# Splitting the first loads over two DMA rings in a fused state-space and gated-MLP kernel

## The chip, the core and the metric

The kernel runs on one core of a Trainium2 chip. The metric is the device time of one execution in microseconds (us): the median of several timed runs. A profile of one further execution shows what each engine did: TensorE (PE for matmuls, PEld for the weight loads ahead of them), VectorE (DVE), ScalarE (ACT), GpSimd (POOL) and SyncE (SP). Two of these, SP and ACT, issue DMAs in this kernel; the rows of the profile call their issue queues SPq and ACTq, and each has a ring of its own that feeds the core's 16 DMA engines.

## What is computed

The input x has 2048 rows of 512 values in bf16. Each row is layer-normalised to xn, and three things are summed:

```
xn  = (x - mean) / sqrt(var + 1e-5)
A   = 2 * Re(scan(xn @ B_bar) @ C) + xn * Dskip      # complex diagonal recurrence over the rows
B   = (silu(xn @ w1) * (xn @ w3)) @ w2               # w1, w3: 512 x 1792; w2: 1792 x 512
out = x + A + B
```

B_bar and the recurrence's factors come from three parameter vectors of 512 values (Lambda_re, Lambda_im, log_dt).

## The kernel before, in words

The rows are cut into four blocks of 512, and each block into four row groups of 128 (`x_blk[b][:, c, :]`). A block passes through four stages on TensorE: `glu_up` (14 feature tiles f of w1 into `g_ps` and of w3 into `u_ps`, four matmuls each, one for each 128-wide slice dt of the 512 input values), `ssm_in`, and `y_out`, while VectorE works through a queue of tasks (normalising, the scan, products) and ScalarE empties PSUM. The order of everything is written by hand (`manual_schedule`): each engine runs its instructions in program order. SP also issues its DMAs in that order. The DMAs take eight completion semaphores in turn, so a DMA that gets a semaphore for the second time is issued only when the DMA before it on that semaphore has landed.

This case is about the first ten microseconds. There the first block has to be made ready in small steps:

- `load_rows` (L77) loads row groups of block 0. Rows 0 to 127 and 128 to 255 (128 KB each) are issued by SP, rows 256 to 511 (256 KB) by ACT.
- `load_w13(0, 4, 2)` (L95, called at L115) loads the columns of feature tiles 0 to 3 of w1 and w3 in four pieces of 256 KB, all on SP: w1 for dt 0 and 1 ("w1 low"), w1 for dt 2 and 3 ("w1 high"), then w3 low and w3 high. After these SP issues the columns of tiles 4 to 7, block 1 of x, the rest of w1 and w3, and so on.
- `load_prm` (L109) loads the three parameter vectors into `prm`, 1 KB each, on ACT.
- `keep_warm` (L150) runs matmuls on a constant; nothing reads their result. There are 8 with 512 columns and 5 with 128 ahead of the first real work, and 2 more with 128 columns between the transposes.
- `stats`, `aggr` (DVE, L164, L167), `rstd_act` (ACT, L171, L172) and `normed` (DVE, L192) normalise one row group; `turn` (PE, L251) transposes it in 128 x 128 pieces, and `put` (L256 on ACT, L258 on DVE) copies the transposed pieces from PSUM to `xnT`. The transposes of row group 1 use the PSUM tiles of feature tile 2 (`t1` is made of `begun[2]`).
- `ahead` (through `glu_mm`, L372) runs the matmuls of feature tiles 0, 1 and 2 on those row groups of block 0 that are ready, before `glu_up` finishes these tiles with the last row group.

On TensorE the order after the first dummies is: transposes of row group 0, two dummies, transposes of row group 1 (four: two low, two high), then

```
ahead((w1_sb,), B3, 0, 1, lo)          # w1 low,  row group 0, tiles 0 to 2: 6 matmuls of 128 columns
ahead((w1_sb,), B3, 1, 1, lo, True)    # w1 low,  row group 1: 6 of 128
ahead((w1_sb,), B3, 0, 2, hi)          # w1 high, row groups 0 and 1: 6 of 256
ahead((w3_sb,), B3, 0, 2, lo)          # w3 low:  6 of 256
turn(2, t2)
ahead((w3_sb,), B3, 0, 2, hi)          # w3 high: 6 of 256
```

followed by the transpose of `prm` (L544), row group 2, the transposes of row group 3, and the rest of `glu_up(0)`.

Of the kernel before, what the change touches and what calls it, by code (L numbers as in the profile page):

```python
# [16 lines left out]
P = 128  # L17
# [3 lines left out]
def kernel(  # L21
# [24 lines left out]
    nc = tc.nc  # L46
# [6 lines left out]
    CPB = TBLK // P  # L53
    NSB = TBLK // SB
    NDT = D // P
# [20 lines left out]
    def load_rows(c0, c1, eng):  # L76
        eng.dma_start(out=x_blk[0][:, c0:c1, :], in_=xv[:, 0, c0:c1, :])  # L77

    load_rows(0, 1, nc.sync)
    load_rows(1, 2, nc.sync)  # L80
    nc.scalar.preload_act_table_set("natural_log_exp_and_others")
    w1_sb = const.tile([P, NDT, F], BF16, name="w1_sb")
    w3_sb = const.tile([P, NDT, F], BF16, name="w3_sb")
    w2_sb = const.tile([P, NFT, D], BF16, name="w2_sb")
    w1v = B_w1.rearrange("(t p) f -> p t f", p=P)
    w3v = B_w3.rearrange("(t p) f -> p t f", p=P)

    H = NDT // 2

    def load_w13(f0, f1, parts=1):  # L90
        fs = slice(f0 * P, f1 * P)
        for w_sb, wv in ((w1_sb, w1v), (w3_sb, w3v)):
            for i in range(parts):
                ds = slice(i * NDT // parts, (i + 1) * NDT // parts)
                nc.sync.dma_start(out=w_sb[:, ds, fs], in_=wv[:, ds, fs])  # L95

    dskip_row = const.tile([P, D], BF16, name="dskip_row")
    bt = [const.tile([P, NDT, PS], BF16, name=f"bt{ri}") for ri in range(2)]
# [9 lines left out]
    def load_prm(i, src, eng):  # L108
        eng.dma_start(out=prm[i * NPT:(i + 1) * NPT, :], in_=src.rearrange("(t p) -> t p", p=P))  # L109

    load_prm(0, A_Lambda_re, nc.scalar)
    load_rows(2, CPB, nc.scalar)
    load_prm(1, A_Lambda_im, nc.scalar)
    load_prm(2, A_log_dt, nc.scalar)
    load_w13(0, 4, 2)  # L115
    load_w13(4, 8)
    nc.sync.dma_start(out=x_blk[1], in_=xv[:, 1, :, :])
    load_w13(8, NFT)
    nc.sync.dma_start(out=dskip_row, in_=A_Dskip.partition_broadcast(P))
    load_turned(bt[0], A_B_re)  # L120
# [26 lines left out]
    def keep_warm(n, width=512):  # L147
        one = nc.const_aps.tensor_like(1.0, like=ident[:, 0:1])
        for _ in range(n):
            nc.tensor.matmul(out=begun[0][0][:, :width], lhsT=one.to_broadcast([P, P]), rhs=one.to_broadcast([P, width]),  # L150
                             start=True, stop=True)

    keep_warm(8)
    keep_warm(5, P)


    mv_all = const.tile([P, NBLK * CPB, 2], FP32, name="mv_all")
# [4 lines left out]
    def stats(c):  # L162
        sums[c] = work.tile([P, 6], FP32, name="stats", bufs=4)
        nc.vector.bn_stats(out=sums[c], in_=x_blk[c // CPB][:, c % CPB, :])  # L164
# [4 lines left out]
    def rstd_act(c0, c1):  # L169
        y = rstd_all[:, c0:c1]  # L170
        nc.scalar.activation(out=y, in_=mv_all[:, c0:c1, 1], func=ACT.Ln, bias=LN_EPS)  # L171
        nc.scalar.activation(out=y, in_=y, func=ACT.Exp, scale=-0.5)  # L172
# [15 lines left out]
    def normed(c, parts=1):  # L188
        xn = work.tile([P, D], BF16, name="xn", bufs=8)
        for i in range(parts):  # L190
            ds = slice(i * D // parts, (i + 1) * D // parts)
            nc.vector.tensor_scalar(out=xn[:, ds], in0=x_blk[c // CPB][:, c % CPB, ds], scalar1=mv_all[:, c, 0:1],  # L192
                                    scalar2=rstd_all[:, c:c + 1], op0=ALU.subtract, op1=ALU.mult)
        return xn
# [54 lines left out]
    def turn(c, pxt, d0=0, d1=NDT):  # L249
        for dt in range(d0, d1):  # L250
            nc.tensor.transpose(out=pxt[:, dt - d0, :], in_=xn0[c][:, dt * P:(dt + 1) * P], identity=ident)  # L251

    def put(c, pxt, eng, d0=0, d1=NDT):
        dst = xnTs[0][:, d0:d1, c * P:(c + 1) * P]
        if eng is nc.scalar:
            nc.scalar.activation(out=dst, in_=pxt, func=ACT.Copy)  # L256
        else:
            nc.vector.tensor_copy(out=dst, in_=pxt)  # L258
# [110 lines left out]
    def glu_mm(b, f, w_sb, ps, ts, dts=range(NDT), joins=False):  # L369

        for dt in dts:
            nc.tensor.matmul(out=ps[:, ts], lhsT=w_sb[:, dt, f * P:(f + 1) * P], rhs=xnTs[b][:, dt, ts],  # L372
                             start=(dt == 0 and not joins), stop=(dt == NDT - 1))
# [128 lines left out]
    def ahead(w_sbs, fs, c, n=1, dts=range(NDT), joins=False):  # L502
        for f in fs:
            for w_sb in w_sbs:
                glu_mm(0, f, w_sb, begun[f][w_sb is w3_sb], slice(c * P, (c + n) * P), dts, joins)
# [13 lines left out]
    xn0[1] = normed(1, 2)  # L519
    turn(0, tb, H, NDT)  # L520
    put(0, tb, nc.scalar, H, NDT)
    keep_warm(2, P)
    turn(1, t1[0], 0, H)
    put(1, t1[0], nc.scalar, 0, H)
    turn(1, t1[1], H, NDT)
    put(1, t1[1], nc.scalar, H, NDT)
    stats(2)
    aggr(2)
    rstd_act(2, 3)
    stats(3)  # L530
    B3 = (0, 1, 2)
    lo, hi = range(H), range(H, NDT)
    ahead((w1_sb,), B3, 0, 1, lo)
    ahead((w1_sb,), B3, 1, 1, lo, True)
    ahead((w1_sb,), B3, 0, 2, hi)
    xn0[2] = normed(2)
    aggr(3)
    rstd_act(3, 4)
    ahead((w3_sb,), B3, 0, 2, lo)
    turn(2, t2)  # L540
    put(2, t2, nc.vector)
    xn0[3] = normed(3)
    ahead((w3_sb,), B3, 0, 2, hi)
    nc.tensor.transpose(out=pprm, in_=prm, identity=ident)  # L544
# [63 lines left out]
```

## Time and profile before

| | |
|---|---|
| median of 3 timed runs | 211.68 us (211.54 to 211.72) |
| the profiled execution | 212.11 us, of which the span from first to last instruction is 210.3 us |
| PE busy | 206.6 us, 98% of the span |
| DVE, ACT, POOL busy | 173.5, 93.4, 6.0 us |
| DMA | 13.69 MB, two rings (q1 is SP's with 13.24 MB, q10 is ACT's with 0.27 MB) |

In rows of the timeline the first number is the start in us from the begin of the span and the second is how long the group of instructions lasted; xN is how many there are. Where a wait preceded, it stands in brackets with what ended it. In the list of DMA issues the last number is the median time from the start of the issue to the landing of the last byte. Matmuls overlap: their starts tell the pace, while the duration of one is longer than the distance to the next.

### The profile page before, as it was taken

The numbers are of one execution on the slowest core, as the hardware profiler recorded it, in microseconds if no ns is written. First come the engines' busy times: TensorE is split into PE (matmuls) and PEld (weight loads), VectorE is DVE, ScalarE is ACT, GpSimd is POOL, SyncE is SP. The second block draws the span as 40 slices with busy tenths as digits, with TensorE's granted clock in tenths as the row PEclk, the third lists the DMA queues.
The fourth block names the chain that finished last, engine by engine and source line by source line (L and its number), as shares of the span: only waits on it lengthen the run. The fifth ranks groups of instructions, "written<-read, shape, count | busy, mean of one in ns | idle before, by whom it ended". The sixth has DMA issues, their size and how long they took to land.

```text
span 210.3 us, 2878 instructions
## 1 busy us (share of the span) xinstructions
PE 206.6 (98%) x1036; PEld 97.7 (46%) x1036; DVE 173.5 (82%) x346; ACT 93.4 (44%) x167; POOL 6.0 (3%) x27
## 2 busy tenths in 40 slices
PE   8999999999999999999999999999999999999994
PEld 3864444444444444444444444444444444444453
DVE  4699989989999999999999999999999999121111
ACT  3599967666666200066666600036666620000000
POOL 2010320000000000000000000000000000000000
PEclk9999999999999999999999999999999999999999
DMA  5999599944000000000004200100000000000110
GB/s 165 294 366 219 109 178 325 217 106 100 0 3 0 0 25 25 28 26 0 0 0 77 28 1 24 50 25 5 0 0 0 0 3 25 27 25 25 34 44 25
DMA packets 25014, 13.69 MB, mean 65 GB/s; under 512 B 15912, under 2 KB 25000, under 8 KB 25000
## 3 DMA queue, kind: packets, MB, share of 16 engines
q1 hardware_dynamic: 24704, 13.24, 26.1%
q10 hardware_dynamic: 296, 0.27, 0.4%
q8 instruction: 8, 0.13, 0.3%
q14 instruction: 6, 0.05, 0.1%
HBM read 7.74 MB, written 2.10 MB: 47 GB/s over the span
## 4 chain that ended last, share of the span: by engine, by line
PE 96%; DMA 2%; SPq 0%; DVE 0%; issue 0%
PE g_ps L372 23%; PE u_ps L372 23%; PE y_ps L488 23%; PE y_ps L493 13%; PE bu_ps L411 13%; DMA w_sb<-in_B_w_dram 2%; SPq L77 0%; PE xt_ps L251 0%; DVE o L498 0%; PE xt_ps L544 0%
## 5 line engine op out<-in xcount | busy, mean ns | idle before, releaser
L372 PEld LDWEIGHTS <-w_sb 128*128 128x128 bf16 x502 | 46.4, 98 | 50.6 <-DMA w_sb<-in_B_w_dram 0.6
L372 PE MATMUL g_ps<-xnT,w_sb 128*128 128x512 bf16 (+2 forms) x254 | 58.2, 354 | 0.3 <-DMA w_sb<-in_B_w_dram 0.3
L372 PE MATMUL u_ps<-xnT,w_sb 128*128 128x512 bf16 (+2 forms) x248 | 58.4, 358 | 0.0
L488 PE MATMUL y_ps<-w_sb,hgT 128*128 128x512 bf16 (+2 forms) x238 | 51.2, 366 | 0.0
L390 ACT ACTIVATE up<-u_ps 128x512 bf16<-128x512 f32 x56 | 34.0, 607 | 14.9 <-PE u_ps L372 14.9
L413 ACT ACTIVATE u<-bu_ps 128x512 bf16<-128x512 f32 x32 | 19.1, 597 | 46.3 <-PE bu_ps L411 46.3
L388 ACT ACTIVATE sl<-g_ps 128x512 bf16<-128x512 f32 x56 | 34.0, 608 | 9.9 <-PE g_ps L372 9.2
L445 DVE TENSOR_TENSOR_SCAN ab<-r_col,h,ab 128x256 bf16<-128x256 f32 x56 | 37.7, 733 | 0.2
L488 PEld LDWEIGHTS <-hgT 128*128 128x128 bf16 x238 | 22.8, 98 | 25.9
L498 DVE TENSOR_TENSOR o<-y_ps,x_blk 128x512 bf16<-128x512 f32 (+2 forms) x17 | 11.1, 654 | 24.3 <-PE y_ps L493 24.3
L493 PE MATMUL y_ps<-ct,h 128*128 128x512 bf16 (+2 forms) x136 | 30.4, 366 | 0.0
L411 PE MATMUL bu_ps<-xnT,bt 128*128 128x512 bf16 x128 | 28.1, 379 | 0.0
L397 DVE TENSOR_TENSOR hgT<-sl,up 128x512 bf16<-128x512 bf16 x56 | 22.9, 414 | 2.1 <-ACT up L390 2.1
L493 PEld LDWEIGHTS <-h 128*128 128x128 bf16 x136 | 13.0, 98 | 14.7
L411 PEld LDWEIGHTS <-bt 128*128 128x128 bf16 x128 | 12.5, 98 | 15.1
L164 DVE BATCH_NORM_STATS2 stats<-x_blk 128x6 f32<-128x512 bf16 x16 | 10.6, 675 | 2.5 <-DMA x_blk<-in_A_x_dram 2.5
L454 DVE TENSOR_TENSOR ab<-ab,tab_s 128x2048 bf16<-128x2048 bf16 x8 | 9.8, 1222 | 0.2
L450 DVE TENSOR_TENSOR ab<-ab,tab_c 128x2048 bf16<-128x2048 bf16 x8 | 9.8, 1222 | 0.1
L427 DVE TENSOR_TENSOR ab<-u,tab_x 128x2048 bf16<-128x2048 bf16 x8 | 9.7, 1219 | 0.0
L430 DVE TENSOR_TENSOR ab<-u,tab_y 128x2048 bf16<-128x2048 bf16 x8 | 9.7, 1218 | 0.0
L201 DVE TENSOR_TENSOR x_blk<-xd,x_blk 128x512 bf16<-128x512 bf16 x16 | 6.8, 426 | 0.5
L200 DVE TENSOR_TENSOR xd<-xn,dskip_row 128x512 bf16<-128x512 bf16 x16 | 6.7, 418 | 0.0
(76 smaller groups left out, 81.3 us busy)
## 6 DMA issues: line engine op xcount, KB each, us to landing
out_dram<-o SPq DMA_DIRECT2D x15, 128.0 KB, 1.7
w_sb<-in_B_w_dram SPq DMA_DIRECT2D x1, 1792.0 KB, 9.3
x_blk<-in_A_x_dram SPq DMA_DIRECT2D x3, 512.0 KB, 6.3
w_sb<-in_B_w_dram SPq DMA_DIRECT2D x2, 768.0 KB, 7.8
w_sb<-in_B_w_dram SPq DMA_DIRECT2D x4, 256.0 KB, 5.0
w_sb<-in_B_w_dram SPq DMA_DIRECT2D x2, 512.0 KB, 4.1
x_blk<-in_A_x_dram SPq DMA_DIRECT2D x2, 128.0 KB, 2.2
x_blk<-in_A_x_dram ACTq DMA_DIRECT2D x1, 256.0 KB, 4.7
```

The costliest lines, as they stand in the source:

```text
L164: nc.vector.bn_stats(out=sums[c], in_=x_blk[c // CPB][:, c % CPB, :])
L372: nc.tensor.matmul(out=ps[:, ts], lhsT=w_sb[:, dt, f * P:(f + 1) * P], rhs=xnTs[b][:, dt, ts], start=(dt == 0 and not joins), stop=(dt == ...
L388: nc.scalar.activation(out=sl16, in_=g_ps, func=ACT.Silu)
L390: nc.scalar.activation(out=up16, in_=u_ps, func=ACT.Copy)
L397: nc.vector.tensor_tensor(out=hg[b][:, f, :], in0=sl16, in1=up16, op=ALU.mult)
L411: nc.tensor.matmul(out=u_ps, lhsT=bt[ri][:, dt, pt * P:(pt + 1) * P], rhs=xnTs[b][:, dt, :], start=(dt == 0), stop=(dt == NDT - 1))
L413: nc.scalar.activation(out=u16[:, :, pt, ri, :], in_=u_ps.rearrange("p (s t) -> p s t", s=NSB), func=ACT.Copy)
L445: nc.vector.tensor_tensor_scan(out=a[:, pt, 2 * ri + 1, :], data0=r_b, data1=a[:, pt, 2 * ri, :], initial=init, op0=ALU.mult, op1=ALU.add)
L450: nc.vector.tensor_tensor(out=a[:, :, 0::2, :], in0=a[:, :, 1::2, :], in1=tab_b("c"), op=ALU.mult)
L488: nc.tensor.matmul(out=y_ps[:, ds], lhsT=hg[b][:, f, cl * P:(cl + 1) * P], rhs=w2_sb[:, f, ds], start=(f == 0), stop=False)
L493: nc.tensor.matmul(out=y_ps[:, ds], lhsT=h_tiles[i][:, pt, ri, h_ts], rhs=ct[ri][:, pt, ds], start=False, stop=(pt == NPT - 1 and ri == 1))
L498: nc.vector.tensor_tensor(out=o16[:, ds], in0=y_ps[:, ds], in1=x_blk[b][:, cl, ds], op=ALU.add)
```

## The change

Rows 128 to 255 are issued by ACT, ahead of its table load, and rows 256 to 511 by SP. ACT's ring then carries the two w1 pieces, SP's the two w3 pieces and after them the three parameter vectors. Five narrow dummies at the start become eight. On TensorE the w1 matmuls of tiles 0 and 1 are done for row group 0 first, the low half of them ahead of the high half of row group 1's transposes; tile 2 comes last, for both row groups at once.

```diff
     load_rows(0, 1, nc.sync)
-    load_rows(1, 2, nc.sync)
+    load_rows(1, 2, nc.scalar)
     nc.scalar.preload_act_table_set("natural_log_exp_and_others")
...
-    load_prm(0, A_Lambda_re, nc.scalar)
-    load_rows(2, CPB, nc.scalar)
-    load_prm(1, A_Lambda_im, nc.scalar)
-    load_prm(2, A_log_dt, nc.scalar)
-    load_w13(0, 4, 2)
+    low, high = slice(0, H), slice(H, NDT)
+    load_w(w1_sb, w1v, 0, 4, nc.scalar, low)
+    load_rows(2, CPB, nc.sync)
+    load_w(w1_sb, w1v, 0, 4, nc.scalar, high)
+    load_w(w3_sb, w3v, 0, 4, nc.sync, low)
+    load_w(w3_sb, w3v, 0, 4, nc.sync, high)
+    load_prm(0, A_Lambda_re, nc.sync)
+    load_prm(1, A_Lambda_im, nc.sync)
+    load_prm(2, A_log_dt, nc.sync)
     load_w13(4, 8)
...
     keep_warm(8)
-    keep_warm(5, P)
+    keep_warm(8, P)
...
     keep_warm(2, P)
     turn(1, t1[0], 0, H)
     put(1, t1[0], nc.scalar, 0, H)
+    ahead((w1_sb,), (0, 1), 0, 1, lo)
     turn(1, t1[1], H, NDT)
     put(1, t1[1], nc.scalar, H, NDT)
     stats(2)
     aggr(2)
     rstd_act(2, 3)
     stats(3)
-    B3 = (0, 1, 2)
-    lo, hi = range(H), range(H, NDT)
-    ahead((w1_sb,), B3, 0, 1, lo)
-    ahead((w1_sb,), B3, 1, 1, lo, True)
-    ahead((w1_sb,), B3, 0, 2, hi)
+    ahead((w1_sb,), (0, 1), 0, 1, hi)
+    ahead((w1_sb,), (0, 1), 1, 1, lo)
+    ahead((w1_sb,), (0, 1), 1, 1, hi)
+    ahead((w1_sb,), (2,), 0, 2)
     xn0[2] = normed(2)
```

`load_w` is the body of the old `load_w13` for one weight, one engine and one half (`eng.dma_start(out=w_sb[:, ds, fs], in_=wv[:, ds, fs])`); B3, lo and hi are defined a few lines earlier.

More of the change, by code (lines that the diff above doesn't have):

```diff
@@ L88, with load_w, load_w13 @@
     H = NDT // 2
-    def load_w13(f0, f1, parts=1):
+    def load_w(w_sb, wv, f0, f1, eng, ds=slice(0, NDT)):
         fs = slice(f0 * P, f1 * P)
[L92 to L95, printed above, removed]
+        eng.dma_start(out=w_sb[:, ds, fs], in_=wv[:, ds, fs])
+    def load_w13(f0, f1):
+        load_w(w1_sb, w1v, f0, f1, nc.sync)
+        load_w(w3_sb, w3v, f0, f1, nc.sync)
     dskip_row = const.tile([P, D], BF16, name="dskip_row")
@@ L521 @@
     put(0, tb, nc.scalar, H, NDT)
+    B3 = (0, 1, 2)
+    lo, hi = range(H), range(H, NDT)
     keep_warm(2, P)
```

## The prediction, made before the result was known

> **What bounds the kernel now.** I read the page first: the span and the chain that ended last.
>
> ```profile
> span 210.3 us, 2878 instructions
> ...
> PE 96%; DMA 2%; SPq 0%; DVE 0%; issue 0%
> ```
>
> The whole time is TensorE's work plus 2% of waiting for one DMA. So I asked for the chain in order of time.
>
> ```profile
> 1.17 0.41 SPq L77
> ...
> 1.64 4.80 DMA w_sb<-in_B_w_dram
> 6.43 0.05 issue
> 6.48 1.51 PE g_ps L372 x18
> 7.99 0.67 PE u_ps L372 x6
> 8.66 0.22 PE xt_ps L251 x4
> ```
>
> The end is set by the landing of w1 low (issued 1.64, landed 6.44); from 6.48 on TensorE runs to the end without a hole. Whatever moves that stream's start, or opens a hole in it, moves the end one for one. Next, what TensorE does before it (timeline):
>
> ```profile
> 4.88 0.65 PE L251 MATMUL xt_ps<-ident,xn 128*128 128x128 bf16 x4
> 5.33 0.42 PE L150 MATMUL g_ps<-const-bfloat16-1.0 128*128 128x128 bf16 x2
> 5.54 0.42 PE L251 MATMUL g_ps<-ident,xn 128*128 128x128 bf16 x2
> 5.76 0.41 PE L251 MATMUL u_ps<-ident,xn 128*128 128x128 bf16 x2
> 6.48 0.62 PE L372 MATMUL g_ps<-xnT,w_sb 128*128 128x128 bf16 x8 [0.31 <-DMA w_sb<-in_B_w_dram]
> ```
>
> Only 0.31 us of idleness is the weights'. The transposes cannot come sooner, because VectorE finishes row group 1 at 5.70 (4.51 + 1.19):
>
> ```profile
> 4.51 1.19 DVE L192 TENSOR_SCALAR xn<-x_blk,mv_all,rstd_all 128x256 bf16<-128x256 bf16 x4
> 6.27 0.69 DVE L164 BATCH_NORM_STATS2 stats<-x_blk 128x6 f32<-128x512 bf16 x1 [0.57 <-DMA x_blk<-in_A_x_dram]
> ```
>
> Last the DMAs, asked for one by one: the issue of rows 256 to 511, the start of w1 high and its time to landing (landing = start + last number), and GB/s by stretches (last column).
>
> ```profile
> x_blk<-in_A_x_dram ACTq DMA_DIRECT2D x1, 256.0 KB, 4.7
> ```
>
> ```profile
> 2.11 0.47 SPq L95 DMA_DIRECT2D w_sb<-in_B_w_dram  x1
> ```
>
> ```profile
> w_sb<-in_B_w_dram SPq DMA_DIRECT2D x1, 256.0 KB, 5.0
> ```
>
> ```profile
> 3.00:3.25 0.25, 0.25 (x2) 0.00 (x0) 0.25 (x1) 0.00 (x0) 0.00 (x0) 1.00 0.24 66
> ...
> 5.00:7.00 2.00, 1.69 (x20) 1.22 (x20) 1.38 (x5) 1.38 (x5) 0.00 (x0) 1.00 1.08 375
> ```
>
> Landings: w1 low 6.44, w1 high 2.11 + 5.0 = 7.11, w3 low 2.62 + 5.2 = 7.82, w3 high 3.40 + 5.0 = 8.40, rows 256 to 511 1.53 + 4.7 = 6.23. TensorE starts w1 high at 7.15 and w3 low at 7.83: each piece is used the moment it lands. From 5 to 7 us the transfers run at 375 GB/s with the engines full; between 3.00 and 4.00 the four stretches show 66, 102, 111 and 250, mean 132.
>
> **The change part by part.**
>
> *Issue.* An issue takes 0.40 to 0.47 us. ACT's first, rows 128 to 255, starts at about 0.72 instead of 1.17 on SP; w1 low follows at 0.72 + 0.44 + 0.05 = 1.21 (was 1.64), w1 high at 1.70 (was 2.11). SP has rows 256 to 511 at 1.17 (was 1.53 on ACT), w3 low at 1.64 (was 2.62), w3 high at 2.1 (was 3.40). So the w1 pieces gain 0.42 us of issue, the w3 pieces 1.0 to 1.3.
>
> *Who shares with whom.* Before, w1 high had 1024 KB to go by its landing: both first row groups, rows 256 to 511, w1 low and itself. Now w3 low is issued beside it on the other ring. Two equal transfers on two rings, rows 256 to 511 and w1 low, were issued 0.11 apart and landed 0.21 apart, so the rings get equal shares, and w1 high shares with 256 KB of w3 low: 262 KB / 375 GB/s = 0.70 us later. Estimate: 7.11 + 0.70 − 0.42 = 7.39. Lower bound: the poor stretch from 3 to 4 us, which loses 1 − 132/375 = 0.65 us, is closed as well: 6.74. Upper bound: the earlier issue brings nothing: 7.81. I take 7.39, since the issue gain is measured and nothing shows that the poor stretch goes away: two rings were in use in it.
>
> The Trainium skill speaks against this edit (DMA: Bandwidth & Descriptors, "Issuing engines are not separate DMA queues"): DMAs of several issuing engines run on the same 16 DMA engines and interleave, and only issue time is saved. The trace agrees: 336 to 373 GB/s from 4 to 5 us with two rings against 375 with one. By the rule the saving is the 0.42 alone, that is my 7.39; the lower bound needs more than it allows.
>
> *Low pieces.* w1 low: 1.21 + 4.8 = 6.0. Rows 256 to 511: 1.17 + 4.7 = 5.9; VectorE's 1.86 us from landing to xn (6.23 to 7.68 + 0.41) then ends at 7.8, before TensorE asks for it. w3 low near 7.4, w3 high near 8.1: both early for the later stream below.
>
> *TensorE's order.* What can run ahead of w1 high shrinks: before, twelve matmuls of 128 columns on w1 low (6.48 to 7.15); now four, then two transposes. What remains behind w1 high grows. Pace: 12 in 0.67 us is 56 ns for 128 columns, 6 in 0.66 is 109 ns for 256. Then: 4 (high, group 0) + 4 (low, group 1) + 4 (high, group 1) = 12 × 0.056 = 0.67, plus tile 2's 4 × 0.109 = 0.44, together 1.11 us. Total columns are unchanged (twenty matmuls for eighteen). The w3 stream so starts at 7.39 + 0.04 + 1.11 = 8.54 instead of 7.83: **+0.7 us**. This is the term that decides. With w1 high at 6.74 it starts at 7.89, no change; at 7.81 it is 8.96, +1.1.
>
> *Second half of group 1.* Its transposes stand behind the four matmuls that wait for w1 low: 6.0 + four at the early pace of 107 ns + two = 6.65; ACT's copy (0.38, L256) ends near 7.3, before its first reader (after w1 high and eight matmuls, 7.9). Hidden; without that cover it would be the next late thing, about 7.1 to 7.3.
>
> *First rows.* Both 128 KB groups now travel together. Alone rows 0 to 127 landed near 2.89; sharing with another 128 KB (0.35 us at 375) costs 0 to 0.35, VectorE's chain moves with it, and the transposes of 4.88 become 4.88 to 5.2. Hidden by the weights' wait; if that cover were gone, up to 0.35.
>
> *Dummies.* Three at 107 ns: 0.32 us. The five started at 4.12 to 4.55, so TensorE was free at 4.66 and stood for 0.22: they push the transposes to 4.98 at most, 0.10 us, under the same cover.
>
> *Table load* on ACT: after one issue, so it ends at 2.43 instead of 2.00; its first user starts at 3.83. Nothing.
>
> *Parameters.* Behind w3 high on SP, the second and third waiting for a first row group's landing (about 3). Issued by 3.6, at 5.2 us to land 8.8; L544 needs them at 9.37, later now. Nothing. Behind them on SP the loads of tiles 4 to 7 wait for landings as before (6.45 now; needed after 14 us, landed by 11.7); block 1 of x moves by perhaps 0.5, has 0.9 of slack at VectorE (landed 13.7, read 14.64).
>
> Sum: +0.7 us. On the profiled execution 212.11 + 0.7 = 212.8; on the median, which is 0.43 lower, 211.68 + 0.65 = **212.3** (rounded to the side of the lower bound, which is the farther one).
>
> **The rivals.** A measurement of this kernel can tell about 0.2%, 0.42 us, from no change.
>
> 1. *The poor stretch closes* and w1 high lands by about 7.1 or sooner. For it: both rings have work queued from 0.7 us, and issues were 0.4 us apart then. Against it: the stretch is poor with two rings. Shift 0 to +0.4: about 211.8.
> 2. *Faster*: w1 low by 5.8 and w1 high by 6.4. Then weights no longer bound. The row chain does: transposes low at 5.54, four matmuls 5.76 to 6.19 at 107 ns, transposes high to 6.40, group 1's second copy done near 7.0, four more, tile 2, w3 at 7.66: −0.17; with the pace of 56 ns from 5.7 on instead of 6.48, −0.5. It decides below w1 high at 6.5, i.e. 0.6 earlier than before with 256 KB more ahead of it. Time 211.2 to 211.5.
> 3. *The fast pace comes late.* Matmuls of 128 columns lasted 311 ns up to the last transposes and 220 ns from 6.48 on: TensorE doubles its pace around there. If it stays slow for 1 us more because TensorE stands waiting for w1 high, 0.5 us is lost beyond the main case: 212.8. The Trainium skill (TensorE: Matmul & The Clock Gate, Part 1) says that the clock is raised after a busy window of about 3.4 us; one such window more would be an estimated 1.7 us, 213.4. No run here shows it.
> 4. *The change does nothing*: w1 high keeps its 7.11 and everything else hides: w3 at 8.26, +0.4. It lies on the border.
>
> **How the numbers follow.** Main case (w1 high after 7.15, shift over 0.42) 0.49, rival 3 within slower 0.03; rivals 1 and 4 together 0.38, rival 2 over the bound 0.10. The likeliest gives 212.3. The range runs from rival 2's near end (211.4) over no change to the upper bound of w1 high, +1.1, with a little of rival 3: 212.9. The main case alone is 212.1 to 212.8.
>
> **What would show it.** Right: in the profile after, a hole ahead of w1's second group of matmuls (L377 there, waiting for a DMA of w_sb) of 0.5 us or more, w1 high and w3 low landing within 0.2 of each other, the first u_ps matmul near 8.5. Wrong: w1 high lands before 6.8, the u_ps stream starts at 7.9 or sooner, or the hole is ahead of the transposes (rows late), or the wait is for ACT's copy.

## The result

The changed kernel takes 212.79 us (median of six runs, 212.49 to 213.33) against 211.70 for the kernel before (six runs, 211.54 to 211.83). The ratio is 1.0052 with a 95% interval of 1.0041 to 1.0064: slower by 1.1 us, where 0.65 was forecast. This is inside the range, and more than forecast.

The page of the changed kernel, span and chain:

```profile
span 211.0 us, 2888 instructions
...
PE 95%; DMA 3%; ACT 0%; ACTq 0%; DVE 0%; issue 0%
```

TensorE's share of the chain falls by one point, the DMA's rises by one. The chain in order of time says which DMA (start, length, what):

```profile
1.67 5.73 DMA w_sb<-in_B_w_dram
7.40 0.04 issue
7.45 1.28 PE g_ps L377 x16
8.73 0.66 PE u_ps L377 x6
```

The DMA issued by ACT at 1.67 is w1 high, no longer w1 low. It lands at 7.40, and 16 matmuls are still to do on w1 behind it. TensorE's timeline shows the hole:

```profile
5.24 0.65 PE L256 MATMUL xt_ps<-ident,xn 128*128 128x128 bf16 x4
...
6.11 0.41 PE L377 MATMUL g_ps<-xnT,w_sb 128*128 128x128 bf16 x4
6.36 0.27 PE L256 MATMUL u_ps<-ident,xn 128*128 128x128 bf16 x2
7.45 1.28 PE L377 MATMUL g_ps<-xnT,w_sb 128*128 128x128 bf16 x16 [0.81 <-DMA w_sb<-in_B_w_dram]
8.56 0.82 PE L377 MATMUL u_ps<-xnT,w_sb 128*128 128x256 bf16 x6
```

Four matmuls on w1 low and the last transposes run early, then TensorE stands for 0.81 us. The w3 stream, which began at 7.83, begins at 8.56, and from there on everything is 0.73 later. The line before:

```profile
7.83 0.83 PE L372 MATMUL u_ps<-xnT,w_sb 128*128 128x256 bf16 x6
```

The transposes of the first row group are late too (4.88, now 5.24), because rows 0 to 127 land later, as VectorE's first line shows, before and after:

```profile
2.89 0.69 DVE L164 BATCH_NORM_STATS2 stats<-x_blk 128x6 f32<-128x512 bf16 x1 [1.96 <-DMA x_blk<-in_A_x_dram]
...
3.25 0.69 DVE L169 BATCH_NORM_STATS2 stats<-x_blk 128x6 f32<-128x512 bf16 x1 [2.32 <-DMA x_blk<-in_A_x_dram]
```

### The profile page after: what moved, and what is told of

Its sections match the earlier page's. It is cut to its first block, busy times and chain, and to the rows that moved or that the text cites. A ratio compares the mean times of both kernels' runs of the same rounds, so it can differ in the third digit from the quotient of the medians.

```text
span 211.0 us, 2888 instructions
## 1 busy us (share of the span) xinstructions
PE 206.8 (98%) x1041; PEld 98.1 (47%) x1041; DVE 173.4 (82%) x346; ACT 93.4 (44%) x167; POOL 6.0 (3%) x27
## 4 chain that ended last, share of the span: by engine, by line
PE 95%; DMA 3%; ACT 0%; ACTq 0%; DVE 0%; issue 0%
PE u_ps L377 23%; PE y_ps L493 23%; PE g_ps L377 23%; PE y_ps L498 13%; PE bu_ps L416 13%; DMA w_sb<-in_B_w_dram 3%; ACT L81 0%; PE xt_ps L256 0%; ACTq L77 0%; DVE o L503 0%; PE xt_ps L551 0%
## 5 line engine op out<-in xcount | busy, mean ns | idle before, releaser
L377 PE MATMUL g_ps<-xnT,w_sb 128*128 128x512 bf16 (+1 forms) x256 | 58.4, 352 | 0.8 <-DMA w_sb<-in_B_w_dram 0.8
```

## The experiments

**Which part of the change costs?** Two kernels take one part each, a third takes the dummies back, and the kernel before is profiled again.

loads_only: the new loads, with TensorE's order and the dummies of before.

```diff
-    keep_warm(8, P)
+    keep_warm(5, P)
...
-    ahead((w1_sb,), (0, 1), 0, 1, lo)      # and the rest of the new order
+    ahead((w1_sb,), B3, 0, 1, lo)          # the old order, as in the kernel before
+    ahead((w1_sb,), B3, 1, 1, lo, True)
+    ahead((w1_sb,), B3, 0, 2, hi)
```

> The new loads, but TensorE's order and the five dummies of before. Main theory (w1 high, landing at 7.40 because it shares with w3 low, sets the start of the w3 stream): behind w1 high only six matmuls of 256 columns remain (0.66 us) instead of 1.11, so the first u_ps matmul starts near 8.1 and the time lies 0.45 below the changed kernel, about 212.35, still above the kernel before. Rival (rows 0 to 127 landing 0.36 later is what costs): the order makes no difference, 212.8. Rival (order alone costs): 211.7.

order_only: the kernel before with the new order alone.

```diff
-    ahead((w1_sb,), B3, 0, 1, lo)          # and the rest of the old order
+    ahead((w1_sb,), (0, 1), 0, 1, lo)      # ahead of turn(1, t1[1], H, NDT)
...
+    ahead((w1_sb,), (0, 1), 0, 1, hi)
+    ahead((w1_sb,), (0, 1), 1, 1, lo)
+    ahead((w1_sb,), (0, 1), 1, 1, hi)
+    ahead((w1_sb,), (2,), 0, 2)
```

> The loads and dummies of before, TensorE's new order. Main theory: w1 high lands at 7.11 as before, 1.11 us of work remain behind it, so the first u_ps matmul starts at about 8.25 instead of 7.83: +0.4, about 212.1. Rival (rows late costs): no rows move, 211.7. Rival (order alone costs it all): 212.8.

five_dummies: the changed kernel with the dummies of before.

```diff
-    keep_warm(8, P)
+    keep_warm(5, P)
```

> The changed kernel with five dummies instead of eight. Main theory: the three dummies fill a wait for rows and stand under the later wait for w1 high: no change, 212.8 within 0.1. Rival (they push the transposes, or their activity sets TensorE's pace): 0.1 to 0.3 off.

before_again has no edit.

> The kernel before, unchanged, for a second profile. If the last of 16 parts of w1 low lands 0.7 us behind the other fifteen in the first profile alone, this profile has w1 low landing near 5.7, the u_ps stream starting 0.3 to 0.4 sooner than 7.83, and about 211.7; if that happens in every execution, 7.83 again and 212.1 with the profile.

| | us, median | runs | ratio to before, interval | w1 high lands | first u_ps matmul |
|---|---|---|---|---|---|
| order_only | 212.09 | 11 | 1.0016 (1.0007 to 1.0025) | 6.3 | 7.69 |
| loads_only | 213.01 | 6 | 1.0053 (1.0032 to 1.0074) | 7.96 | 8.67 |
| five_dummies | 212.96 | 4 | 1.0065 (1.0050 to 1.0079) | 7.6 | 8.77 |
| before_again | 211.54 | 1 | | 6.3 | 7.28 |

The order alone costs 0.37 of the 0.4 expected, but not by the path that was expected. In its profile w1 high landed at 6.34 and not at 7.11, TensorE waited for no weight, and the first u_ps matmul came at 7.69 and not at 8.25:

```profile
6.38 1.47 PE L372 MATMUL g_ps<-xnT,w_sb 128*128 128x128 bf16 x16
7.69 0.82 PE L372 MATMUL u_ps<-xnT,w_sb 128*128 128x256 bf16 x6
```

So the agreement of the time is no proof of the theory, and what in the order costs is open. The dummies cost nothing that these runs resolve. loads_only is a miss: the loads alone cost as much as the whole change, and the old order gave nothing back. The surprise is before_again. Its chain does not start with a weight:

```profile
0.72 2.06 DMA x_blk<-in_A_x_dram
2.78 0.02 issue
2.81 0.70 DVE stats L164
...
5.96 1.48 PE g_ps L372 x18
7.44 0.66 PE u_ps L372 x6
```

In this execution the rows set the pace: row group, `stats`, `normed`, transposes, copies. w1 low landed at 1.64 + 4.0 = 5.6 and not at 6.44, and the u_ps stream began at 7.28 (timeline) and not at 7.83:

```profile
7.28 0.82 PE L372 MATMUL u_ps<-xnT,w_sb 128*128 128x256 bf16 x6
```

In the trace of the first profile the landing of w1 low has sixteen parts; fifteen had arrived by 5.67 and the last at 6.43. Rows 256 to 511 and the other three pieces had the same one late part, 0.7 to 0.8 behind the rest. before_again has no such part. The first profile, of an execution of 212.11 us where the medians are 211.7, showed one disturbed start.

The start of the u_ps stream can be turned into time. In the nine profiles of the two kernels, their repeats, order_only, loads_only, loads_again, five_dummies and copy_on_dve (three of them come below), the time of the profiled execution less this start is 204.26 to 204.28 us. A median of 211.70 so belongs to a start at about 7.43, and 212.79 to one at about 8.52.

**Is the traffic beside w1 high what makes it late?** Repeats of two kernels and two edits, side by side.

> The changed kernel, unchanged, beside the next three: 212.8, w1 high landing between 7.3 and 7.7, the first u_ps matmul at 8.5 to 8.8.

> The new loads with TensorE's order and five dummies of before, once more, because its six runs lay between 211.98 and 213.77. Main theory (the wait for w1 high, and what is left to do behind it): 0.45 below the changed kernel, 212.35. Rival (the old order brings nothing, because w3 low or w3 high then is what TensorE waits for): equal to the changed kernel, 212.8, with holes ahead of the u_ps matmuls.

w3_late holds everything that SP loads after the rows and the parameters:

```diff
-    load_w(w3_sb, w3v, 0, 4, nc.sync, low)     # and all later loads of SP: moved below
...
     stats(0)
     aggr(0)
+    held = const.tile([P, 2], FP32, name="held")
+    nc.sync.dma_start(out=held, in_=mv_all[:, 0, :])
+    load_w(w3_sb, w3v, 0, 4, nc.sync, low)
+    load_w(w3_sb, w3v, 0, 4, nc.sync, high)
```

> The changed kernel, but SP issues the parameters first and holds the two w3 pieces and all later loads back behind a tiny DMA that waits for the first aggr (about 4.2). Main theory (w1 high is late because w3 low shares the DMA engines with it): w1 high lands 0.7 sooner or more, near 6.2, the w3 stream starts near 8.0, and the time falls by 0.5 to 0.7, to about 212.2. Rival (ACT's ring is slow by itself, or one straggling engine sets w1 high whatever runs beside it): w1 high still after 7.2, 212.8.

w3low_act is the kernel before with w3 low on the other ring:

```diff
     load_rows(2, CPB, nc.scalar)
+    nc.scalar.dma_start(out=w3_sb[:, :H, :4 * P], in_=w3v[:, :H, :4 * P])
     load_prm(1, A_Lambda_im, nc.scalar)
```

> The kernel before with one DMA moved: w3 low goes to ACT's ring, behind rows 256 to 511, so that it runs beside w1 high. Main theory (sharing): w1 high, at 6.34 in a typical execution of before, lands at 7.0, its matmuls start at 7.05 instead of 6.62: +0.4, about 212.1. Rival (the new loads cost by late rows and not by sharing): no change, 211.7.

| | us, median (range) | runs | ratio to before, interval | w1 high lands | first u_ps matmul |
|---|---|---|---|---|---|
| after_again | 213.04 (212.54 to 215.44) | 11 | 1.0075 (1.0046 to 1.0104) | 7.4 | 8.54 |
| loads_again | 213.09 (212.26 to 215.36) | 9 | 1.0069 (1.0033 to 1.0105) | 8.3 | 9.00 |
| w3_late | 212.43 (212.24 to 212.77) | 12 | 1.0028 (1.0018 to 1.0038) | 6.1 | 8.19 |
| w3low_act | 215.16 (214.77 to 215.82) | 5 | 1.0156 (1.0133 to 1.0179) | 7.6 | 10.8 |

With only rows 256 to 511 and the parameters on SP's ring, w1 high needs 4.4 us from issue to landing instead of 5.7:

```profile
w_sb<-in_B_w_dram ACTq DMA_DIRECT2D x1, 256.0 KB, 4.4
```

So the traffic on the other ring is what delays it, by 1.3 us here. The edit holds back w3 low, w3 high and tiles 4 to 7 together, so it does not say how much each of them does. Of the time, 0.4 to 0.6 us is won back (against the eight runs of after_again at full clock, whose median is 212.82, and against all eleven) and 0.7 remains. w3_late has no hole at w1 high any more. One is ahead of the first transposes, which start at 5.55 (4.80 in before_again):

```profile
5.55 0.65 PE L247 MATMUL xt_ps<-ident,xn 128*128 128x128 bf16 x4 [0.37 <-DVE xn L188]
```

The other is the edit's own: w3 low, issued at 5.09 behind the tiny DMA, landed at 8.14, and its first reader started 0.05 later, about 0.15 later than the pace of the matmuls ahead of it would have had it. So the 0.7 that remains is not the rows alone:

```profile
w_sb<-in_B_w_dram SPq DMA_DIRECT2D x1, 256.0 KB, 3.0
...
8.19 0.83 PE L368 MATMUL u_ps<-xnT,w_sb 128*128 128x256 bf16 x6
```

loads_again repeats the miss. Its lowest runs (212.26 there, 211.98 in loads_only) lie 0.3 to 0.5 below the lowest of the changed kernel (212.54, 212.49), as expected of the old order when w1 high comes early. The thirteen runs of these loads at full clock (0.999 or more) fall into two groups, six at 211.98 to 212.56 and seven at 212.94 to 213.77; the fourteen of the changed kernel lie between, at 212.49 to 213.33. Both profiles are of the upper group: w1 high landed at 8.0 to 8.3 and not at 7.4 to 7.6, with the same DMAs issued at the same times. The unevenness is in the last of its sixteen parts. In the five profiles with w3 beside it the eighth part landed at 6.3 to 6.6, but the last 0.95 to 2.0 us after it; in before_again the eighth came at 5.92 and in w3_late at 5.60, and the last 0.4 to 0.5 after it. Why the last parts trail so unevenly is open.

w3low_act is a miss (215.16 for 212.1), and it cannot be read by its time. The extra DMA shifted the semaphores, so that ACT's last `load_prm` waited for w1 low, and `rstd_act` was queued behind it on ACT (timeline of ACT):

```profile
6.20 0.28 ACTq L109 DMA_DIRECT2D prm<-in_A_log_dt_dram  x1
6.52 0.20 ACT L174 ACTIVATE rstd_all<-mv_all 128x1 f32<-128x1 f32 x1 [4.52 <-DMA w_sb<-in_B_w_dram]
```

Its landing can be read: w1 high at 2.11 + 5.5 = 7.6 (7.57), with w3 low on the other ring, against 2.10 + 4.2 = 6.3 (6.34): 1.2 later. What the long hole did to TensorE's clock stands in the last section.

**What the rows cost.** late_old_order is w3_late with the old order (the diff of loads_only, with eight dummies). late_rows_back is w3_late with

```diff
-    load_rows(1, 2, nc.scalar)
+    load_rows(1, 2, nc.sync)
...
+    load_prm(0, A_Lambda_re, nc.scalar)
     load_w(w1_sb, w1v, 0, 4, nc.scalar, low)
...
-    load_prm(0, A_Lambda_re, nc.sync)
```

and w1_own_ring is late_rows_back with the old order. copy_on_dve is a try to beat both kernels:

```diff
-    put(1, t1[0], nc.scalar, 0, H)
+    put(1, t1[0], nc.vector, 0, H)
```

> The kernel w3_late (the new loads, w3 and all later loads held back until the first aggr) with TensorE's order of before. Theory of three parts: w3 low beside w1 high costs about 0.5, late rows 0.3, the new order 0.4. Then only the late rows are left: about 212.05, the first u_ps matmul 0.3 sooner than w3_late's 8.19 (w3 low, landing at 8.1 there, may then be the wait). Rival (the order costs only by what it puts behind a late w1 high): no change, 212.4.

> The kernel w3_late with rows 128 to 255 back on SP behind rows 0 to 127, and the first parameter vector on ACT ahead of w1, so that w1 low is issued at about 1.5 as before; TensorE's new order. Theory of three parts: the rows land at 2.8 and 3.3 again, the transposes start near 4.85 instead of 5.55, and only the order is left: 212.1. Rival (the row chain is covered by the weights): no change, 212.4.

> All three parts taken back but the ring: w1's two pieces on ACT's ring, rows on SP's as before, w3 held back, TensorE's order of before, eight dummies. Theory of three parts: within 0.2 of the kernel before, 211.6 to 212.0, w1 high before 6.4. Rival (a DMA on ACT's ring is slow in itself): 212.3 or more.

> The kernel before with one copy moved: the first half of row group 1 from PSUM to xnT on VectorE instead of ScalarE. In an execution of before without a late engine, w1 is there early, and TensorE stands 0.16 us for that copy (between four and more matmuls at 6.0). If the row chain is what bounds the kernel before, this brings 0.1 to 0.15: 211.6. If the weights bound it, nothing.

| | us, median | runs | ratio to before, interval | first stats | first u_ps matmul | hole ahead of w3 high |
|---|---|---|---|---|---|---|
| late_old_order | 212.39 | 6 | 1.0029 (1.0018 to 1.0040) | 3.59 | 8.20 | none |
| late_rows_back | 212.85 | 6 | 1.0050 (1.0039 to 1.0062) | 2.94 | 7.71 | 0.49 |
| w1_own_ring | 212.59 | 5 | 1.0042 (1.0029 to 1.0055) | 2.98 | 7.51 | 0.51 |
| copy_on_dve | 211.70 | 11 | 0.9998 (0.9990 to 1.0007) | 2.83 | 7.43 | none |

By their times the first three are misses. The traces say why. With the rows on one ring again, the first `stats` comes 0.6 us sooner than in w3_late, and the u_ps stream 0.48 sooner (7.71 against 8.19); the weight loads of w1 high had to wait there too, for its landing at 6.55. Then a new wait follows, w3 high:

```profile
7.71 0.82 PE L368 MATMUL u_ps<-xnT,w_sb 128*128 128x256 bf16 x6
...
9.25 0.83 PE L368 MATMUL u_ps<-xnT,w_sb 128*128 128x256 bf16 x6 [0.49 <-DMA w_sb<-in_B_w_dram]
```

Its issue had waited for rows 256 to 511 (landed 1.64 + 4.21 = 5.85), whose semaphore it reuses. The chain of late_rows_back:

```profile
1.64 4.21 DMA x_blk<-in_A_x_dram
5.85 0.02 issue
5.87 3.33 DMA w_sb<-in_B_w_dram
```

So the row term, about half a microsecond, is shown by the stream's start and not by the time, and a part of this half may be TensorE's pace, which rose at another moment in these profiles (last section). In late_old_order w3 low landed at 8.15, just ahead of the u_ps stream, so it could not show what the order is worth. w1_own_ring took the time that its rival forecast, but ACT's ring is not shown to be slow in itself: with w3 held back, w1 high needed 4.1 to 4.6 us on it, against 4.2 on SP's ring in before_again. copy_on_dve shows no difference; the 0.1 that it was to bring lies inside its interval. No version run here is shown to beat the kernel before.

## Why the prediction held, point by point

**The deciding term.** "The w3 stream so starts at 7.39 + 0.04 + 1.11 = 8.54": measured 7.40 and 8.56. The hole is where it was expected. w3_late and w3low_act show that traffic on the other ring makes w1 high late, by 1.2 to 1.3 us. The work behind w1 high was right: 8.56 − 7.45 = 1.11.

**But 7.39 came out of two errors that cancel.** I let the poor stretch from 3 to 4 us stay. It closed; the four quarters now show 332, 356, 328 and 332 GB/s, as in

```profile
3.00:3.25 0.25, 0.25 (x2) 0.00 (x0) 0.00 (x1) 0.00 (x0) 0.00 (x0) 1.00 0.97 332
```

and w1 low landed at 1.19 + 3.8 = 5.0 instead of the 6.0 of the sum, rows 256 to 511 at 4.8 instead of 5.9, w3 low at 1.64 + 4.7 = 6.3 instead of 7.4. w1 high alone did not profit. I had w1 high and w3 low land together; they landed 1.1 apart, in the order that hurts. In the trace fifteen of w1 high's sixteen parts had landed by 6.63 and the last came at 7.40. The 7.11 that the sum started from held such a part as well: fifteen by 6.34, the last 0.77 later. So the agreement to 0.01 us is luck: it sets one start with a late part against another. What stands is the direction and the typical landing: in after_again w1 high came at 7.38 without a single late part, the last six of sixteen between 6.90 and 7.38. The sum counts the bytes ahead of w1 high; how far the last of its parts trails, which is what TensorE waits for, was no term of it. The signs of being right were met in the hole and the u_ps start, and missed in w3 low. The "375 with one" ring is no clean row either: rows 256 to 511, on ACT's ring, landed at 6.23, within that stretch. Rival 1 was right about the stretch and wrong about what follows from it.

**The size that was off is the start before.** The sum took 7.83 for the w3 stream and said +0.7. The profile pair agrees: 8.56 − 7.83 = 0.73. The medians differ by 1.09, because a usual execution of before starts the stream earlier (7.28 in before_again, 7.43 in copy_on_dve, whose time is the median's) and has spare time on the weights: in before_again w1 high lands at 6.3 and its matmuls, those of 256 columns, start at 6.62. "Each piece is used the moment it lands" held for one disturbed execution. The profiled execution lay 0.4 above the median; I carried that offset through as if it belonged to both kernels. Rounding to the lower bound then went the wrong way.

**The rows.** Priced at 0 to 0.35 and "hidden by the weights' wait". The first `stats` came at 3.25 to 3.6 in the profiles of the new loads, against 2.8 to 2.9: 0.4 to 0.75. It is hidden only while w1 high is later still; in w3_late the hole ahead of the transposes stands in the open, beside the late w3 low.

**The edits costed at nothing.** Table load, parameters and tiles 4 to 7 ended no wait of TensorE in the profile of the changed kernel. The dummies: no change within the interval, as said. ACT's second copy (6.67 + 0.38) was done before w1 high, as said.

**The rivals.** "Faster" needed w1 high by 6.5; w3_late has it at 6.1 and is still slower than before; the late rows are the next bound there, and then w3 low, which the edit itself delays. How the 1.1 us divide over sharing, rows and order is not shown, because the terms cover one another. Rival 3, the late fast pace, showed itself in another form (last section).

## What to carry to other kernels

Before a profiled wait is taken as the bound, hold the profiled execution's time against the median: 0.4 us above it was the sign here that the wait belonged to that execution. Moving loads to a second ring started them sooner here, but the first transfer, on which everything hangs, then shared with its neighbour (rows 0 to 127 came 0.4 to 0.75 us later), and the piece that was needed next shared with the piece that could wait (w1 high came 1.0 to 2.0 us later than in before_again). A DMA is waited for until its last part is there, so look at the parts and not at the bytes alone. Where work is reordered, count what is left behind the last arrival; and where completion semaphores are reused in turn, each DMA moved also moves who waits for whom.

## What the runs showed of the hardware that was not expected

**TensorE's clock falls after a hole.** In w3low_act TensorE stood for 2.53 us ahead of its transposes. The stretches of its profile (length, PE busy, granted clock, DMA share, GB/s):

```profile
5.00:8.60 3.60, 1.20 (x14) 1.00 1.08 363
8.70:10.00 1.30, 1.30 (x11) 0.50 1.10 352
10.00:12.00 2.00, 2.00 (x11) 0.50 1.10 352
12.10:14.00 1.90, 1.90 (x30) 1.00 1.07 373
```

Half the clock for 3.3 to 3.5 us, after the work had come back: about 1.7 us lost. The 18 matmuls from 8.29 to the u_ps stream took 2.50 us, against 1.48 in before_again, and what follows the stream's start took 204.90 us instead of 204.26: 1.02 and 0.64. The Trainium skill (TensorE: Matmul & The Clock Gate, Part 1) says that the clock is set by how busy TensorE was in a free-running window of about 3.4 us; the length agrees. The hole itself was shorter, 2.53 us. One of the five runs of w3low_act, of 214.77 us, kept a mean clock of 1.000 and was only 0.35 to 1.05 us shorter than the four at 0.991 to 0.992, so the times of the runs do not confirm the 1.7 that the profile shows. Three of the eleven runs of after_again took 214.68, 214.95 and 215.44 us at a mean granted clock of 0.990 to 0.992, while the other eight, at 1.000, took 212.54 to 213.22; two of the nine of loads_again did the same (215.28 and 215.36 at 0.991 to 0.992). 0.9% of 213 us is 1.9 us, so one such window fits them. None of these five was profiled, so that a hole ahead of the weights caused them is argued and not shown. No run of the kernel before fell below 0.998.

**One part of a DMA can lag.** In the first profile of before, one of sixteen parts came 0.7 to 0.8 us behind the others for five transfers in a row, and in the second not at all. In the profiles of the changed kernel and of five_dummies w1 high had such a part (6.63 to 7.40, 6.84 to 7.61), and the two w3 pieces had not. What held it is not settled.

**TensorE's pace rises at another time in each execution.** A matmul of 128 columns lasted about 311 ns up to 5.9 us in the first profile of before and 219 from 6.5 on; in other profiles the change came between 6.1 and 6.7 us (the changed kernel, after_again, w3_late, late_old_order, order_only, copy_on_dve), between 4.1 and 4.6 (loads_only, loads_again, w1_own_ring), or before 4.1 (before_again, late_rows_back). So a part of the 0.55 us between the u_ps starts of the two profiles of before is the pace and not the late part; how much is not shown.
